# wo·w_in formed once on the chip; u and v taken from the 256 gated attention features; wo summed in the output's PSUM

## The chip, the cores and the metric

One core of one Trainium2 chip runs the whole kernel as one program. The metric is the device time of one execution in microseconds (us). TensorE (PE in the profile) multiplies, VectorE (DVE), ScalarE (ACT) and GpSimd (POOL) work element by element, and SyncE's queue (SP) issues nearly all DMAs. Each engine takes its instructions in the order in which they stand in its own queue; engines wait for one another by semaphores.

## The reference, cut to what matters

Eight batches of S = 576 tokens; D = 512 model features, E = 4 experts (heads) of 64, so 256 gated features per token.

```python
x = rmsnorm(q @ (k.T @ v)) * g_norm                  # 8 heads of 64 -> x[b] is 576 x 512
# attention over 4 experts, causal, top-2 gates w:
#   y[b] = sum_e w_e * softmax(mask(x wq_e (x wk_e)^T / 8)) (x wv_e) @ wo[e]
x2 = concat_e(w_e * a_e @ (x wv_e)) @ wo             # (576 x 256) @ (256 x 512)
h = gelu_tanh(x2 @ w_in)                             # (576 x 512) @ (512 x 1024)
u, v = h[:, :512], h[:, 512:]
vn = layernorm(v) * g_ln
gated = u * (w_sg @ vn + b_sg)                       # w_sg mixes the 576 tokens
out = x2 + gated @ w_out                             # (576 x 512) @ (512 x 512)
```

w_in and w_out arrive as 64-bit floats and are taken apart on the chip.

## The kernel before, in words

**Split products.** Nearly every matrix product takes three matmuls with fp32r operands: an operand is split into a rounded part (hi: a copy on ScalarE) and the rest (lo: a subtraction on VectorE or GpSimd), and hi·hi, hi·lo and lo·hi are summed in PSUM. Below, "a product" of 128 x 128 weights is three matmuls. A half row is 288 tokens.

**Phase 1** (class Phase1) runs per batch: front (the k·v products and the norm's sums, `kvps`, `outps`, `statps`), norm (`nps`), v and gates (`vps`), q and k (`qkps`), then attn: per head e = 0..3 and query block i = 0..4 scores (`scps`, L433 and L434), masked row minimum on VectorE (L436), exp on ScalarE (L448), transposes (`tps`, L483), their split (L491 ScalarE, L493 VectorE), `av` (`avps`, L510), and after each second head the gating of `gav` and its split into `gvh` (L530) and `gvl` (L531). `wo_out` (L534) multiplies these 256 gated features by wo (L543 to L545; 48 matmuls a batch), copies PSUM to `x2ev` on ScalarE (L546) and writes x2 to DRAM (`x2d`). The tag x2ev has two buffers and is shared by `x2ev` and by the `avt` of `av`.

**Order.** Each part is a generator with a time window in units of one batch's attention, relative to its batch (OPT["w"]: attn 0 to 1, wo 1.102 to 1.366, that is, during the next batch's first heads). `merge` calls the generators by these times, and a scheduler then sets each engine's order from this text order and its own estimate of times. The generator conv takes w_in, w_sg and w_out apart in pieces of 128 x 256 and stores hi and lo in DRAM over about six batches. Batch 7's attention is accompanied by `first` of Phase2.

**Phase 2** (class Phase2) takes the batches in pairs. `load_x` reads x2 back (`xraw`) and splits it (L739 ScalarE, L740 GpSimd). `upart` makes u over 512 features (L791 to L793; 96 matmuls a batch with 288 columns), `vpart` makes v in nine blocks of 128 tokens for a pair (L841 to L843; 108 matmuls a pair with 512 columns), each followed by gelu, batch statistics and `vnorm`. `spart` mixes tokens (L867 to L871; 112 a batch), multiplies by u and splits the result into `gh` and `gl`. `opart` multiplies by w_out (L899 to L901; 96 a batch), adds x2 read back once more (`xres`, L902) and writes the output. The weights of this phase lie where phase 1 keeps its attention tiles, so `Phase2.weights` can load them only when these are free.

Of the kernel before, what the change touches and what calls it, by code (L numbers as in the profile page):

```python
# [16 lines left out]
try:  # L17
# [17 lines left out]
P = 128  # L35
# [8 lines left out]
OPT = dict(ob=1, sx=0, pinq=0, dv=0, pin=1, cvb=2, xb=1, ldb=2, hp={}, n1=0, n2=0, f1=0, pa=4, sA=(), dg=0, cost=(1.01, 0.88, 1.22, 1.47, 1.28), avi=1, prb=4, ahb=2, alb=2, qkb=2, ahead=3, w={'attn': (0.0, 1.0), 'wo': (1.102, 1.366), 'qk1': (-0.013, 0.222), 'qk0': (-0.54, -0.204), 'v': (-0.683, -0.28), 'front': (-1.386, -0.923), 'norm': (-0.832, -0.787), 'conv': (0.032, 6.648), 'wts': (-1.938, -1.178), 'u': (0.319, 1.263), 'front_0': (-1.763, -1.646), 'v_0': (-1.478, -1.291), 'qk0_0': (-1.025, -0.914), 'qk1_0': (-0.003, 0.152), 'norm_0': (-1.6, -1.5)})  # L44
# [9 lines left out]
    "wo": [("attn", 0)],  # L54
# [12 lines left out]
class Phase1:  # L67
# [6 lines left out]
    def __init__(self, tc, late, early, ins, wts, x2d, nb):  # L74
        self.tc, self.nc, self.nb, self.x2d, self.wts = tc, tc.nc, nb, x2d, wts
        (self.qT, self.kvp, self.gn, self.wqkvg, self.wo, self.sel, self.bsel, self.mask, self.ident) = ins
# [58 lines left out]
    def consts(self):  # L135
# [24 lines left out]
        self.wohi = self.ac.tile([P, 2, D], F32R, name="wohi")  # L160
        self.wolo = self.ac.tile([P, 2, D], F32R, name="wolo")
# [3 lines left out]
    def weights(self):  # L165
        nc = self.nc
        for st, (n0, n1) in zip(self.stg, ((512, 772), (0, 256), (256, 512))):
            for c in range(NC):
                self.split(st[:, c, :], self.whi[:, c, n0:n1], self.wlo[:, c, n0:n1], -0.125 if n0 == 0 else None)
                yield 1.0  # L170
        nc.sync.dma_start(self.mask_sb, self.mask)
        nc.sync.dma_start(self.id_sb, self.ident)
        st = self.staging(2 * D).rearrange("p (r n) -> p r n", r=2)
        nc.sync.dma_start(st, self.wo.rearrange("(r p) n -> p r n", p=P))
        for r in range(2):
            self.split(st[:, r, :], self.wohi[:, r, :], self.wolo[:, r, :])
            yield 2.0
# [317 lines left out]
    def av(self, st, e):  # L495
# [7 lines left out]
        t = self.at.tile([P, S], F32, name="avt", tag="x2ev", bufs=2)  # L503
# [15 lines left out]
        if e % 2:  # L519
# [12 lines left out]
            st["gv"].append((hi, lo))  # L532

    def wo_out(self, b, st, c):  # L534
        nc = self.nc
        ev = self.at.tile([P, S], F32, name="x2ev", tag="x2ev", bufs=2)
        for h in range(2):
            r = slice(HF * h, HF * (h + 1))
            ps = self.bank("wops", True)[:, 0:HF]
            for k in range(2):  # L540
                hi, lo = st["gv"][k]
                wh, wl = self.wohi[:, k, c * P : (c + 1) * P], self.wolo[:, k, c * P : (c + 1) * P]
                nc.tensor.matmul(ps, wh, hi[:, r], start=(k == 0), stop=False)  # L543
                nc.tensor.matmul(ps, wh, lo[:, r], start=False, stop=False)
                nc.tensor.matmul(ps, wl, hi[:, r], start=False, stop=(k == 1))  # L545
            nc.scalar.copy(ev[:, r], ps)  # L546
        nc.sync.dma_start(self.x2d[b][c], ev)

    def attn(self, b, st):
        st["prob"], st["aT"], st["gv"], st["den"], st["R"] = {}, {}, [], [], []  # L550
# [3 lines left out]
        for n in range(len(steps) + ahead):  # L554
# [4 lines left out]
            if n >= ahead:  # L559
# [4 lines left out]
                if i == OPT["avi"] and e > 0:  # L564
                    with self.hp("a"):
                        self.av(st, e - 1)
                    yield 1.0
        self.av(st, E - 1)
        yield 1.0

    def wo_all(self, b, st):
        for c in range(NC):
            self.wo_out(b, st, c)
            yield 1.5
# [14 lines left out]
    def convert(self, w, src, hi_d, lo_d, rows, n):  # L589
        nc = self.nc  # L590
        new = lambda nm, dt, tag=None: self.cv.tile([P, 256], dt, name=nm, tag=tag or nm)[:, :n]
        if src.dtype == I64:
            x = new("cv_x", F32)
            xv = x[:rows]
            low, high = w[:rows, :, 0], w[:rows, :, 1]
            t = x.bitcast(U32)
            h, f = new("cv_h", U32), new("cv_f", F32)
            self.pin(nc.scalar.activation(f, low, AF.Copy, scale=2.0**-52))
            self.pin(
                nc.vector.tensor_scalar(t, high, 3, 0x3FFFFFF8, op0=OP.logical_shift_left, op1=OP.bitwise_and)  # L600
            )
            yield
            nc.vector.scalar_tensor_tensor(h, high, 0xC0000000, t, op0=OP.bitwise_and, op1=OP.bitwise_or)
            yield
            nc.vector.tensor_scalar(t, high, 0x7FFFFFFF, None, op0=OP.bitwise_and)
            yield
            nc.vector.scalar_tensor_tensor(
                x, t, float(897 << 20), h.bitcast(F32), op0=OP.is_ge, op1=OP.mult
            )
            yield  # L610
            nc.vector.tensor_scalar(h, t, 0xFF800000, None, op0=OP.bitwise_and)
            yield
            nc.gpsimd.tensor_tensor(f, f, h.bitcast(F32), op=OP.mult)
            nc.gpsimd.tensor_tensor(x, x, f, op=OP.add)
            yield
        else:
            xv = w[:rows]
            yield
        hi, lo = new("cv_hi", F32R, "cv_h"), new("cv_lo", F32R, "cv_f")
        self.pin(nc.scalar.copy(hi[:rows], xv))  # L620
        self.pin(nc.gpsimd.tensor_tensor(lo[:rows], xv, hi[:rows].bitcast(F32), op=OP.subtract))
        nc.sync.dma_start(hi_d.bitcast(F32), hi[:rows].bitcast(F32))
        nc.sync.dma_start(lo_d.bitcast(F32), lo[:rows].bitcast(F32))
        yield

    def conversions(self):
        units = []
        for src, hi, lo in self.wts:
            r, n = src.shape
            w = 192 if n == S else 256  # L630
            for r0 in range(0, r, P):
                r1 = min(r, r0 + P)
                for n0 in range(0, n, w):
                    n1 = min(n, n0 + w)
                    units.append([t[r0:r1, n0:n1] for t in (src, hi, lo)] + [r1 - r0, n1 - n0])
# [15 lines left out]
    def streams(self):  # L651
# [19 lines left out]
        prep.append((*w["wts"], 16.0, self.weights()))  # L671
# [18 lines left out]
class Phase2:  # L690


    def __init__(self, tc, ctx, ins, wts, x2d, out, nb):
        self.tc, self.nc, self.nb, self.x2d, self.out = tc, tc.nc, nb, x2d, out
        (self.g_ln, self.b_sg), (self.wi, self.ws, self.wo) = ins, wts
        left = lambda name, bufs, **kw: ctx.enter_context(tc.tile_pool(name=name, bufs=bufs, side="left", **kw))
        self.cu = left("m_cu", 1)
        self.xp = left("m_x", 1)
        self.up = left("m_u", 2)
        self.tp = left("m_t", 2)  # L700
        self.ps1 = left("m_ps1", 8 - OPT["pa"], space=PSUM)
        self.wih, self.wil = [], []

    def late(self, ctx):
# [3 lines left out]
        self.vp = right("m_v", 1)  # L708
        self.rp = right("m_r", 2)
# [6 lines left out]
    def load_wi(self, f):  # L716
        for lst, nm in ((self.wih, "h"), (self.wil, "l")):
            lst.append(self.cu.tile([P, NC, D], F32R, name=f"wi{nm}{f}"))
        for c in range(NC):
            for t, src in zip((self.wih[f], self.wil[f]), self.wi):  # L720
                self.move(t[:, c, :], src[c * P : (c + 1) * P, D * f : D * (f + 1)])
            yield 0.75

    def load_x(self, b):

# [303 lines left out]
```

## Time and profile before

| what | value |
|---|---|
| time, median of 3 runs | 979.5 us (977.41 to 980.55) |
| the profiled execution, its own time | 983.26 us |
| its span, first to last instruction | 981.4 us |
| mean granted TensorE clock | 0.979 |
| TensorE matmul busy | 926.1 us, 94% |
| VectorE busy | 551.6 us, 56% |
| ScalarE busy | 524.5 us, 53% |
| GpSimd busy | 372.1 us, 38% |
| DMA, mean over the span | 127 GB/s |

Busy shares are means over the span; phase 1 ends at about 573 us with the last `gvh`, and the shares on the two sides of it differ. The granted clock is a share of full speed. Matmuls are pipelined: the duration of one row overlaps the next row, so the cost of one in a dense stretch is the distance between starts.

### The profile page before, as it was taken

The page shows a single profiled execution, that of the slowest core. Times are in us where ns is not written, and L with a number is a line of the kernel's source. Part 1 is how long each engine was busy: PE and PEld are TensorE (multiplying, and loading weights), DVE is VectorE, ACT ScalarE, POOL GpSimd, SP SyncE. Part 2 cuts the span into 40 slices and gives each one's busy share as a digit, 9 for nine tenths or more (in the row PEclk, how much of TensorE's full clock was granted, in tenths as well). Part 3 has the DMA queues.
Part 4 walks back from the last instruction along what each step waited for, and adds up shares of the span by engine and source line. Part 5 has one row for each costly group of instructions (what it writes and reads, how often), then busy time and mean ns, then how long its engine had stood idle before and what let it go on. Part 6 is the DMA issues. An engine that isn't in the chain of part 4 may idle for free.

```text
span 981.4 us, 18531 instructions
## 1 busy us (share of the span) xinstructions
PE 926.1 (94%) x6592; PEld 877.0 (89%) x6592; DVE 551.6 (56%) x1551; ACT 524.5 (53%) x1386; POOL 372.1 (38%) x390
## 2 busy tenths in 40 slices
PE   5687999999899999999999998999999999999998
PEld 4577988899798988999898987998999999999998
DVE  4565868868797667887975527335222541246022
ACT  5376777677787868778756737213331243115200
POOL 0043555535454545456423313622172125323111
PEclk9698999999999999999999999999999999999999
DMA  9274563673654756634468118512032302330022
GB/s 278 79 196 116 142 197 111 198 211 108 179 169 142 217 155 190 188 112 134 129 161 291 34 41 275 156 54 74 1 105 90 97 1 63 108 97 2 1 95 76
DMA packets 79758, 124.41 MB, mean 127 GB/s; under 512 B 11489, under 2 KB 38945, under 8 KB 79666
## 3 DMA queue, kind: packets, MB, share of 16 engines
q1 hardware_dynamic: 79426, 122.83, 42.5%
q8 instruction: 53, 0.87, 0.4%
q0 software_dynamic: 240, 0.39, 0.2%
q14 instruction: 39, 0.32, 0.1%
HBM read 67.05 MB, written 27.82 MB: 97 GB/s over the span
## 4 chain that ended last, share of the span: by engine, by line
PE 73%; DVE 9%; ACT 8%; DMA 5%; issue 3%; SPq 2%; POOL 0%; ACTq 0%; DVEq 0%
PE avps L510 4%; PE ps L867 4%; PE ps L791 3%; PE ps L793 3%; PE ps L901 3%; PE ps L869 3%; PE ps L900 3%; PE ps L899 3%; PE ps L792 3%; PE ps L868 3%; PE ps L841 3%; PE ps L842 3%; PE ps L843 3%; PE tps L483 3%; PE qkps L297 3%
## 5 line engine op out<-in xcount | busy, mean ns | idle before, releaser
L448 ACT ACTIVATE prob<-prob,small 128x128 f32<-128x128 f32 (+4 forms) x160 | 97.7, 612 | 30.6 <-DVE small L436 28.9
L879 DVE TENSOR_TENSOR g<-ps,u 128x288 f32<-128x288 f32 (+2 forms) x80 | 30.3, 395 | 136.9 <-PE ps L871 136.8
L436 DVE CUSTOM_DVE_ANT_0 prob<-scps,mask_sb 128x128 f32<-128x128 f32 (+4 forms) x160 | 75.2, 478 | 40.1 <-PE scps L434 38.1
L493 DVE TENSOR_TENSOR aTl<-tps,aTh 128x384 fp32r<-128x384 f32 (+1 forms) x192 | 78.2, 431 | 20.0 <-ACT aTh L491 19.6
L883 POOL TENSOR_TENSOR gl<-g,gh 128x576 fp32r<-128x576 f32 x32 | 45.8, 1432 | 109.1 <-ACT gh L882 109.0
L882 ACT CAST gh<-g 128x576 fp32r<-128x576 f32 x32 | 21.6, 674 | 110.1 <-DVE g L879 109.8
L483 PE MATMUL tps<-id_sb,prob 96*128 96x96 f32 (+2 forms) x480 | 73.0, 263 | 6.4 <-ACT x2ev L546 3.3
L297 PE MATMUL qkps<-xhi,whi 128*128 128x288 f32 x256 | 78.3, 306 | 0.6 <-DVE bdl L212 0.4
L867 PE MATMUL ps<-wsh,vnh 128*128 128x288 f32 x256 | 75.4, 297 | 3.0 <-ACT wsl L763 3.0
L298 PE MATMUL qkps<-xlo,whi 128*128 128x288 f32 x256 | 76.5, 299 | 0.0
L299 PE MATMUL qkps<-xhi,wlo 128*128 128x288 f32 x256 | 76.1, 297 | 0.0
L793 PE MATMUL ps<-xh,wil 128*128 128x288 f32 x256 | 75.5, 296 | 0.0
L869 PE MATMUL ps<-wsh,vnl 128*128 128x288 f32 x256 | 75.5, 295 | 0.0
L792 PE MATMUL ps<-xl,wih 128*128 128x288 f32 x256 | 75.4, 296 | 0.0
L868 PE MATMUL ps<-wsl,vnh 128*128 128x288 f32 x256 | 75.3, 294 | 0.0
L901 PE MATMUL ps<-gh,wo2l 128*128 128x288 f32 x256 | 75.3, 295 | 0.0
L791 PE MATMUL ps<-xh,wih 128*128 128x288 f32 x256 | 74.4, 296 | 0.9 <-ACT xh L739 0.9
L900 PE MATMUL ps<-gl,wo2h 128*128 128x288 f32 x256 | 75.1, 294 | 0.0
L491 ACT CAST aTh<-tps 128x384 fp32r<-128x384 f32 (+1 forms) x192 | 68.9, 389 | 11.5 <-PE tps L483 10.6
L899 PE MATMUL ps<-gh,wo2h 128*128 128x288 f32 x256 | 73.7, 294 | 0.0
L433 PE MATMUL scps<-kh,qs 128*128 128x128 f32 (+2 forms) x192 | 64.8, 344 | 8.7 <-DMA kh<-hiT 4.0
L740 POOL TENSOR_TENSOR xl<-xraw,xh 128x576 fp32r<-128x576 f32 x32 | 46.6, 1461 | 63.6 <-ACT xh L739 59.3
(171 smaller groups left out, 3092.8 us busy)
## 6 DMA issues: line engine op xcount, KB each, us to landing
kv<-in_kvp SPq DMA_DIRECT2D x30, 384.0 KB, 4.1
kh<-hiT SPq DMA_DIRECT2D x64, 144.0 KB, 2.8
kl<-loT SPq DMA_DIRECT2D x64, 144.0 KB, 2.8
x2d<-x2ev SPq DMA_DIRECT2D x32, 288.0 KB, 2.8
xres<-x2d SPq DMA_DIRECT2D x32, 288.0 KB, 3.0
out<-oev SPq DMA_DIRECT2D x32, 288.0 KB, 2.2
q<-in_qT SPq DMA_DIRECT2D x30, 288.0 KB, 4.0
kv<-in_kvp SPq DMA_DIRECT2D x30, 192.0 KB, 4.3
```

The source lines that it names most:

```text
L297: nc.tensor.matmul(ps, whi, xhi, start=(c == 0), stop=False)
L448: nc.scalar.activation(sc[:m, 0:w], sc[:m, 0:w], AF.Exp, bias=mn, scale=-1.0, accum_out=den)
L483: nc.tensor.transpose(ps[:kr, m * j : m * j + m], pr[:m, _first(j) : _first(j) + kr], self.id_sb[:m, :m])
L791: nc.tensor.matmul(ps, wh, xh[:, c, :], start=(c == 0), stop=False)
L792: nc.tensor.matmul(ps, wh, xl[:, c, :], start=False, stop=False)
L793: nc.tensor.matmul(ps, wl, xh[:, c, :], start=False, stop=(c == NC - 1))
L867: nc.tensor.matmul(ps, vnh[:, j, fs], self.wsh[:, j, r], start=(j == 0), stop=False)
L868: nc.tensor.matmul(ps, vnh[:, j, fs], self.wsl[:, j, r], start=False, stop=False)
L869: nc.tensor.matmul(ps, vnl[:, j, fs], self.wsh[:, j, r], start=False, stop=False)
L899: nc.tensor.matmul(ps, wh, gh, start=(f == 0), stop=False)
L900: nc.tensor.matmul(ps, wh, gl, start=False, stop=False)
L901: nc.tensor.matmul(ps, wl, gh, start=False, stop=(f == NC - 1))
```

## The change

- `wo_out`, `wo_all`, their window and `x2d` go. `av` now writes `gvh` and `gvl` to DRAM (`gvd`), four transfers a batch, and `avt` has its own tag with two buffers.
- `conv` takes w_in apart as before, but keeps four fp32 pieces (`cv_x4`), multiplies them by the transposed wo (`wot`) in full fp32 (`wxps`, 32 matmuls with 256 columns in all), and stores hi and lo of the 256 x 1024 product. wo itself is split by the same generator (four pieces more).
- Phase 2 loads `gvh` and `gvl` as `xh` and `xl`, with no split. u and v now contract over 256 features: 48 matmuls a batch and 54 a pair. `opart` sums wo's six product terms and w_out's twelve in one PSUM bank (144 matmuls a batch) and copies it out; nothing is added or read back.
- `first` now makes the nine v blocks of batches 0 and 1 unprocessed (`raw`), then u of batch 0. After phase 1 come `vnorm` of these blocks and u of batch 1. `rest` then interleaves `spart` of b, `opart` of b - 1, v of the next pair and u of b + 1 step by step; vn has three buffers.
- The window of u is 0.25 to 1.0 (before 0.319 to 1.263), that of wts ends earlier.

The diff, cut to its core (conv's bit handling, loads and `vnorm` read as before):

```diff
-            st["gv"].append((hi, lo))
-    def wo_out(self, b, st, c):
...
-                nc.tensor.matmul(ps, wh, hi[:, r], start=(k == 0), stop=False)
-                nc.tensor.matmul(ps, wh, lo[:, r], start=False, stop=False)
-                nc.tensor.matmul(ps, wl, hi[:, r], start=False, stop=(k == 1))
-            nc.scalar.copy(ev[:, r], ps)
-        nc.sync.dma_start(self.x2d[b][c], ev)
+            for t, dst in zip((hi, lo), self.gvd[b]):
+                nc.sync.dma_start(dst[e // 2].bitcast(F32), t.bitcast(F32))
...
+            yield from self.whole(w, self.x4[:, c, :], rows)
+            if c < NC - 1:
+                return
+            for r in range(2):
+                rs = slice(r * P, (r + 1) * P)
+                ps = self.bank("wxps")[:, 0:256]
+                for j in range(NC):
+                    nc.tensor.matmul(ps, self.wot[:, j, rs], self.x4[:, j, :], start=(j == 0), stop=(j == NC - 1))
+                self.parts(ps, hi_d[rs, n0 : n0 + 256], lo_d[rs, n0 : n0 + 256], P, 256, psum=True)
...
+            for k in range(2):
+                wh, wl = self.wih[0][:, k, cols], self.wil[0][:, k, cols]
+                nc.tensor.matmul(ps, wh, xh[:, k, r], start=(k == 0), stop=False)
+                nc.tensor.matmul(ps, wh, xl[:, k, r], start=False, stop=False)
+                nc.tensor.matmul(ps, wl, xh[:, k, r], start=False, stop=(k == 1))
...
+            terms = [(self.woh[:, k, cs], self.wol[:, k, cs], xh[:, k, r], xl[:, k, r]) for k in range(2)]
+            terms += [
+                (self.wo2h[:, f, cs], self.wo2l[:, f, cs], gh[:, r], gl[:, r]) for f, (gh, gl) in enumerate(self.g[b])
+            ]
+            for n, (wh, wl, gh, gl) in enumerate(terms):
+                nc.tensor.matmul(ps, wh, gh, start=(n == 0), stop=False)
+                nc.tensor.matmul(ps, wl, gh, start=False, stop=False)
+                nc.tensor.matmul(ps, wh, gl, start=False, stop=(n == len(terms) - 1))
+            (nc.scalar.copy if h else nc.vector.tensor_copy)(ev[:, r], ps)
...
+        for k in range(9):
+            ps = self.vmat(0, k)
+            (nc.vector.tensor_copy if k % 2 else nc.scalar.copy)(self.raw[:, k, :], ps)
...
+        for k in range(9):
+            self.vnorm(0, k, self.raw[:, k, :])
+            if k in (1, 3, 5, 7):
+                f = k // 2
+                self.upart(1, f)
```

The scheduler's order moves with it. TensorE, batch 7's second head, before: its scores and transposes (`scps`, `tps`) have `wops` of batch 6 and the first u matmuls (`ps`) between them.

```order
L434 MATMUL scps<-kl_7714,qs_7519 128x128
L544 MATMUL wops<-gvl,wohi 128x288
L545 MATMUL wops<-gvh,wolo 128x288
L544 MATMUL wops<-gvl,wohi 128x288
L545 MATMUL wops<-gvh,wolo 128x288
L483 MATMUL tps<-id_sb,prob 128x128 x3
L543 MATMUL wops<-gvh,wohi 128x288
```

TensorE, the same head after the change:

```order
L428 MATMUL scps<-kl_7312,qs_7114 128x128
L477 MATMUL tps<-id_sb,prob 128x128 x3
L427 MATMUL scps<-kh_7311,qs_7114 128x256
L428 MATMUL scps<-kl_7312,qs_7114 128x256
L477 MATMUL tps<-id_sb,prob 128x96 x4
L427 MATMUL scps<-kh_7311,qs_7114 128x384
L428 MATMUL scps<-kl_7312,qs_7114 128x384
```

Nothing stands between the steps now, from the last q and k matmul in head 0 to the end of head 2; there the first v block (`ps` from `xh` and `wih`) begins.

TensorE after the change, where phase 1 has ended: the last v block that is made ahead (for batch 2) and the start of `spart` of batch 0, which reads the newly loaded `wsh` and `wsl` and the normed `vn`.

```order
L812 MATMUL ps_8634<-wil_7683,xh 128x512
L813 MATMUL ps_8634<-wih_7680,xl 128x512
L867 MATMUL ps_8425<-wsh,vn 128x288
L867 MATMUL ps_8441<-wsh,vn 128x288
L867 MATMUL ps_8488<-wsh,vn 128x288
L867 MATMUL ps_8504<-wsh,vn 128x288
L868 MATMUL ps_8425<-wsl,vn 128x288
```

Between the last matmul of the attention and these rows stand 24 u matmuls of batch 1 and 24 v matmuls of batch 2; before the change all 108 v matmuls of the first pair lie around this place.

TensorE after the change, one of the eight places of the new product in phase 1 (`wxps`, two groups of four matmuls for each 256 columns):

```order
L520 MATMUL rps<-id_sb,R 128x128
L610 MATMUL wxps<-cv_x_849,wot 128x256 x4
L520 MATMUL rps<-id_sb,R 128x96 x2
L427 MATMUL scps<-kh_1439,qs_1194 128x128
```

Its operand `cv_x` is the fourfold piece `cv_x4`; ahead of it and behind it stand the attention's own transposes and scores.

## Rows read from the trace of the kernel before

**Rows 1.** The page: busy us of each engine, share, instructions.
```profile
PE 926.1 (94%) x6592; PEld 877.0 (89%) x6592; DVE 551.6 (56%) x1551; ACT 524.5 (53%) x1386; POOL 372.1 (38%) x390
```
**Rows 2.** Stretches: length, then busy (count) of PE, PEld, DVE, ACT, POOL; clock, DMA.
```profile
0.00:120.00 120.00, 92.66 (x607) 83.25 (x608) 70.47 (x218) 70.49 (x197) 33.87 (x44) 0.90 0.57 161
120.00:520.00 400.00, 380.12 (x2882) 359.64 (x2881) 311.42 (x966) 299.90 (x884) 197.52 (x206) 0.98 0.58 164
520.00:600.00 80.00, 75.62 (x505) 70.31 (x504) 35.69 (x95) 49.69 (x122) 20.53 (x22) 0.98 0.42 139
600.00:960.00 360.00, 360.00 (x2473) 346.41 (x2472) 129.28 (x261) 103.09 (x183) 117.04 (x118) 1.00 0.24 74
```
**Rows 3.** TensorE in order of time, dense stretches: start, duration, what.
```profile
583.83 0.29 PE L543 MATMUL wops<-gvh,wohi 128*128 128x288 f32 x1
...
584.23 0.30 PE L543 MATMUL wops<-gvh,wohi 128*128 128x288 f32 x1
...
590.91 0.39 PE L841 MATMUL ps<-wih,xh 128*128 128x512 f32 x1
...
592.27 0.39 PE L841 MATMUL ps<-wih,xh 128*128 128x512 f32 x1
```
**Rows 4.** TensorE in order of time: fp32 products, transposes, and what follows each.
```profile
300.38 1.28 PE L206 MATMUL kvps<-kv 128*128 128x128 f32 x10
301.42 0.38 PE L297 MATMUL qkps<-xhi,whi 128*128 128x288 f32 x1
...
319.86 1.28 PE L483 MATMUL tps<-id_sb,prob 128*128 128x128 f32 x12
320.92 0.48 PE L247 MATMUL statps<-sqh,sel_sb 128*16 128x288 f32 x2
```
**Rows 5.** Who waited for whom: us, times, longest; then one such wait in time.
```profile
ACT x2ev L546 <- DMA x2d<-x2ev: 9.8, 6, 2.8
...
349.80 0.70 ACT L546 COPY x2ev<-wops 128x288 f32<-128x288 f32 x2 [2.79 <-DMA x2d<-x2ev]
...
350.25 0.44 PE L483 MATMUL tps<-id_sb,prob 128*128 128x128 f32 x2 [1.56 <-ACT x2ev L546]
```
**Rows 6.** Two stretches around that wait, columns as in rows 2.
```profile
345.00:350.00 5.00, 3.57 (x25) 3.10 (x24) 4.37 (x14) 2.21 (x6) 2.85 (x2) 1.00 0.93 245
350.00:355.00 5.00, 4.75 (x25) 4.65 (x26) 1.80 (x4) 3.15 (x8) 3.85 (x4) 0.66 0.26 99
```
**Rows 7.** ScalarE: the last gvh of batches 0 and 6.
```profile
132.88 0.66 ACT L530 CAST gvh<-gav 128x576 fp32r<-128x576 f32 x1
...
516.96 0.66 ACT L530 CAST gvh<-gav 128x576 fp32r<-128x576 f32 x1
```
**Rows 8.** Groups by line: busy, mean ns of one, idle before, releasers.
```profile
L448 ACT ACTIVATE prob<-prob,small 128x128 f32<-128x128 f32 (+4 forms) x160 | 97.7, 612 | 30.6 <-DVE small L436 28.9 <-DVE gden L364 0.7
L493 DVE TENSOR_TENSOR aTl<-tps,aTh 128x384 fp32r<-128x384 f32 (+1 forms) x192 | 78.2, 431 | 20.0 <-ACT aTh L491 19.6
L436 DVE CUSTOM_DVE_ANT_0 prob<-scps,mask_sb 128x128 f32<-128x128 f32 (+4 forms) x160 | 75.2, 478 | 40.1 <-PE scps L434 38.1 <-ACT prob L448 1.0
L491 ACT CAST aTh<-tps 128x384 fp32r<-128x384 f32 (+1 forms) x192 | 68.9, 389 | 11.5 <-PE tps L483 10.6
L448 ACT ACTIVATION_READ_ACCUMULATOR prob<-prob,small 128x1 f32 (+1 forms) x160 | 31.3, 196 | 0.0
L546 ACT COPY x2ev<-wops 128x288 f32<-128x288 f32 x64 | 23.7, 398 | 21.7 <-DMA x2d<-x2ev 9.8 <-PE wops L545 7.7 <-PE nps L282 2.5
```
**Rows 9.** The start of phase 2's weights and of spart, in order of time.
```profile
587.26 0.33 SPq L752 DMA_DIRECT2D glb<-in_g_ln  x1
...
596.80 1.30 PE L867 MATMUL ps<-wsh,vnh 128*128 128x288 f32 x4 [3.01 <-ACT wsl L763]
...
601.55 0.29 PE L868 MATMUL ps<-wsl,vnh 128*128 128x288 f32 x1
```

More of the change, by code (lines that the diff above doesn't have):

```diff
@@ L627, in conversions @@
         units = []
[L628 removed]
+        src, hi, lo = self.wts[0]
+        for n0 in range(0, 2 * D, 256):
+            for c in range(NC):
+                units.append([src[c * P : (c + 1) * P, n0 : n0 + 256], hi, lo, P, 256, (c, n0)])
+        for src, hi, lo in self.wts[1:]:
             r, n = src.shape
@@ new lines, in vmat @@
+    def vmat(self, p, k):
+        nc = self.nc
+        if k == 4:
+            (xh, xl), r = self.ends[p], slice(0, P)
+        else:
+            (xh, xl), j = self.x[2 * p + (k > 4)], k - 5 * (k > 4)
+            r = slice(j * P, (j + 1) * P)
+        ps = self.bank(self.ps1, "ps1")
+        for c in range(2):
+            wh, wl = self.wih[1][:, c, :], self.wil[1][:, c, :]
+            nc.tensor.matmul(ps, xh[:, c, r], wh, start=(c == 0), stop=False)
+            nc.tensor.matmul(ps, xh[:, c, r], wl, start=False, stop=False)
+            nc.tensor.matmul(ps, xl[:, c, r], wh, start=False, stop=(c == 1))
+        return ps
@@ new lines, in rest @@
+    def rest(self):
+        nb = self.nb
+        self.load_x(2)
+        self.load_x(3)
+        for k in range(9):
[3 more added lines that the diff above has]
+                self.upart(1, f)
+                ins = self.nc.scalar.activation(self.u[0][:, f, :], self.u[0][:, f, :], AF.Gelu_apprx_tanh)
+                self.tc.keep_in_program_order(ins)
+        for b in range(nb):
+            units = [(self.spart, b, 0)]
+            if b:
+                units += [(self.opart, b - 1, c) for c in range(NC)]
+            units += [(self.spart, b, f) for f in range(1, NC)]
+            p = b // 2 + 1
+            steps = []
+            if 2 * p < nb:
+                steps += [(n, self.vstep, p, k) for n, k in enumerate(range(4) if b % 2 == 0 else range(4, 9))]
+            if 0 < b < nb - 1:
+                steps += [(n + 0.5, self.upart, b + 1, f) for n, f in enumerate(range(NC))]
+            steps.sort(key=lambda t: t[0])
+            done = 0
+            for n, (fn, *args) in enumerate(units):
+                fn(*args)
+                if fn == self.opart and args[1] == NC - 1:
+                    self.load_x(b + 3)
+                while done < len(steps) * (n + 1) / len(units):
+                    _, step, *rest = steps[done]
+                    step(*rest)
+                    done += 1
+        for c in range(NC):
+            self.opart(nb - 1, c)
@@ L948, in fused_kernel, with vstep @@
+    def vstep(self, p, k):
+        if k == 0:
+            self.load_ends(p)
+        self.vnorm(p, k, self.vmat(p, k))
 @with_exitstack
-def fused_kernel(ctx, tc, qT, kvp, gn, wqkvg, wo, w_in, g_ln, w_sg, b_sg, w_out, sel, bsel, mask, ident, out):
+def fused_kernel(ctx, tc, qT, kvp, gn, wqkvg, woT, wo, w_in, g_ln, w_sg, b_sg, w_out, sel, bsel, mask, ident, out):
     nb = qT.shape[0]
     dp = ctx.enter_context(tc.tile_pool(name="x2dram", bufs=1, space=DRAM))
-    x2d = [dp.tile([NC, P, S], F32, name=f"x2d{b}") for b in range(nb)]
+    gvd = [[dp.tile([2, P, S], F32R, name=f"gv{x}{b}") for x in "hl"] for b in range(nb)]
@@ L960, in fused_kernel @@
     early.close()
-    ph2 = Phase2(tc, mlp, (g_ln, b_sg), [w[1:] for w in wts], x2d, out, nb)
+    ph2 = Phase2(tc, mlp, (g_ln, b_sg), [w[1:] for w in wts], gvd, out, nb)
     lo, hi = (nb - 1 + t for t in OPT["w"]["u"])
-    live = [[lo, step, gen] for lo, step, gen in left] + [[lo, (hi - lo) / 27.0, ph2.first()]]
+    live = [[lo, step, gen] for lo, step, gen in left] + [[lo, (hi - lo) / 19.2, ph2.first()]]
     merge([(lo, lo + step, 1.0, gen) for lo, step, gen in live])
```

431 lines of the change are left out of this document (179 added, 252 removed).

## The prediction

> **What bounds the kernel now.** First the page: TensorE's matmuls are busy for 94% of the span, VectorE and ScalarE for 56% and 53% [rows 1]. A mean over two phases says little, so next the busy time by stretches [rows 2]. From 600 to 960 us TensorE has no idle time at all, and the other engines are busy for about a third: phase 2 is TensorE's work and nothing else. From 120 to 520 us, inside phase 1, TensorE is busy 380.1 of 400 us, but VectorE 311.4 and ScalarE 299.9: it leads, with VectorE at 78% not far behind, and its clock is 0.98 of full speed. So a matmul removed in phase 2 is worth its full cost; one removed in phase 1 is worth it only as far as the queues can close the gap. Third, TensorE in order of time for the real cost of a matmul: three with 288 columns start within 0.40 us, six with 512 columns within 1.36 us [rows 3], so 0.133 and 0.227 us each.
>
> **The change, part by part.** All sums are made against the profiled execution (983.3 us, 1.9 us more than its span). It lies 3.8 us above the median of the runs, which I take off at the end.
>
> *Matmuls.* The wo product of phase 1 goes: 8 x 48 = 384 at 0.133, -51.2 us. u halves from 96 to 48 a batch: 384, -51.2. v halves from 108 to 54 a pair: 216 at 0.227, -49.0. The output product grows from 96 to 144 a batch: 384, +51.2. The new product is full fp32. The only fp32 products in the trace are `kvps`, where a matmul makes two rows: five matmuls of 128 columns take 1.04 us to the next start [rows 4], 1.63 ns a column. 32 x 256 = 8,192 columns make +13.3. Net: -86.9 us, of which -37.9 in phase 1 (wo and the new product) and -49.0 in phase 2.
>
> *Element work.* `x2ev` copies (64), the load splits (32 on ScalarE, 32 on GpSimd) and the residual's transfers go; 64 output copies replace the adds. In phase 2 this is hidden under TensorE, which has no idle time there [rows 2], so 0 both ways; uncovered, it would cost what the page's idle engines have to spare, and they have two thirds. In phase 1 ScalarE loses 23.7/8 = 3.0 us a batch [rows 8].
>
> *A stall that goes.* ScalarE waited 9.8 us in six pieces for `x2d` transfers to free `x2ev`; in the one shown, 2.79 us of it left TensorE idle for 1.56 us [rows 5] and the clock at 0.66 in the next 5 us [rows 6], about 1.6 us more. At that rate all six would be worth 11 us, at the least 0; I take -5. What is late next: `gvh` and `gvl` now wait for their own transfers, but each has two buffers and is made twice a batch, some 30 us apart, so nothing. SP's queue carries as many stores for them as for `x2d` (four a batch); for the weights it gets 16 stores fewer of the product than of w_in, and 4 loads and 8 stores more of wo: even, 0.
>
> *Phase 1 with less to fill it.* A batch takes (516.96 - 132.88)/6 = 64.0 us [rows 7]. TensorE is busy for 60.8 of it, and 60.8 - 6.4 + 1.9 (the new product, over seven batches) = 56.3 remains. If it is idle for 5% as now, a batch takes 59.3 us, with VectorE at 49.8 us (84%). The wo matmuls stood in the next batch's first heads as work that needs nothing from that attention, and the new product waits for a chain of ScalarE, VectorE and GpSimd; the scores behind it wait too. So I take 7% idle, 60.5 us: +1.2 x 7 = +8.5. Bounds: 0 (5% stays) and +33 (a batch stays at 64 us).
>
> *Batch 7's heads 0 to 2.* There the new order has no other work on TensorE. A head needs 3,712 score columns and 3,264 of `avps` at 0.133/288, 3.2 us, and 15 transposes at 1.06/12 [rows 4], 1.3: 4.5 us. ScalarE needs (97.7 + 31.3 + 68.9)/32 = 6.2 us a head, VectorE (75.2 + 78.2)/32 = 4.8, each before `av`'s evictions [rows 8]. 2.5 such heads leave TensorE idle for about 4 us more than before; with waits between the steps I take +5. Bounds: 0, and +16 if these 11 us of matmuls run at half clock besides.
>
> *The seam.* `spart` needs the newly loaded w_sg. Before, the first one began 9.5 us after the issue of `glb`, and the second operand was in use after 14.3 us; v matmuls covered all but 3.0 us of it [rows 9]. Now the cover behind the attention's last matmul is 24 x 0.133 + 24 x 0.227 = 8.6 us, and `glb` is issued about 2 us after that matmul, behind the last `gvh` and `gvl`: 16.3 - 8.6 is nearly 8 us idle, +5 against before. Bounds: +2 (GpSimd's part shorter, loads sooner) and +10 (with a lowered clock behind it). The extra changes of ScalarE's table in head 3 (gelu, exp, gelu) lie beside 18.6 us of v and u matmuls: 0, at the most +3.
>
> Sum: 983.3 - 86.9 - 5 + 8.5 + 5 + 5 = 909.9; less 3.8, **906 us**.
>
> [...]
>
> **The rivals.**
> *Full gain.* The scheduler fills what wo leaves, idle stays at 5%, the heads and the seam cost 2 us each: 983.3 - 86.9 - 5 + 4 - 3.8 = 892. For it: ScalarE gets lighter and the stall goes. Against it: the order shows the empty stretch of batch 7.
> *Phase 1 does not shrink.* VectorE's chain or the waiting product sets the pace, and a batch stays at 64 us: +33 instead of +8.5, 931 us. For it: in rows 6 VectorE is busy for 4.37 of 5 us while TensorE waits. Against it: over 400 us VectorE has 22% to spare [rows 2].
> [...]
> *It does not do what it says.* Excluded by the new order: 5,864 matmuls instead of 6,432, as counted above.
>
> **How the numbers follow.** The forecast (897 to 916) has 0.52; the full gain (below 897) 0.2; phase 1 that shrinks little or not (917 to 935) 0.24; slower 0.03; the remaining 0.01 lies between. No range can be told from no change within 0.3%, about 3 us; all cases but the last two are faster by far more, hence 0.96, 0.01, 0.03. The range 890 to 926 leaves out about 2 in 10, mostly above.
>
> **What would show it.** The part of phase 2 behind the seam should take about 33 us less: there 312 u matmuls and 186 v matmuls go (-41.5 and -42.2 us) and 384 of the output come (+51.2). If TensorE shows idle time there, the step "worth its full cost" is wrong. A batch between last `gvh` rows should be near 60 us; 64 means the third case, 58 the full gain. `wxps` rows should start 1.6 ns a column apart, with TensorE's idle time ahead of them under 1 us each. In heads 0 to 2 of batch 7 TensorE should be busy for about 60%, with the clock between 0.66 and 1. Between the last `gvh` and the first `spart` matmuls there should be about 8 us of idle time, released by w_sg's transfer or by `vn`. I would be wrong most of all if the granted clock of phase 1 falls below 0.95, or if VectorE has no idle time there.

## The result, and the profile after

The changed kernel takes 950.96 us (median of 4 runs, 946.42 to 954.41) beside 979.76 us (4 runs): a ratio of 0.9707, 95% interval 0.9657 to 0.9757. It is faster by 29 us; 74 were forecast, and the time lies above the range. All rows below are of its profiled run (946.42 us, span 944.6). The two profiled runs (983.26 and 946.42 us) lie 36.8 us apart, 8 more than the medians, so these rows show the change somewhat better than it is.

The page's line on the engines and its row of granted clocks in 40 equal slices of the span; the first answers to [rows 1]:
```profile
PE 863.8 (91%) x6056; PEld 808.5 (86%) x6056; DVE 540.9 (57%) x1513; ACT 500.8 (53%) x1321; POOL 317.0 (34%) x346
...
PEclk9699997988989999998999999799999999999999
```
Stretches, columns as in [rows 2]: inside phase 1, the seam, and phase 2 behind the last `gvh`.
```profile
120.00:520.00 400.00, 358.52 (x2547) 329.14 (x2546) 302.84 (x928) 274.86 (x801) 182.62 (x186) 0.94 0.53 150
...
580.00:592.80 12.80, 7.50 (x40) 6.20 (x38) 3.73 (x7) 7.46 (x15) 3.14 (x5) 1.00 0.68 213
...
580.10:944.60 364.50, 352.42 (x2513) 344.79 (x2511) 127.94 (x240) 111.61 (x209) 91.08 (x103) 0.99 0.18 60
```
ScalarE in order of time, the last `gvh` of batches 0, 6 and 7, as in [rows 7]:
```profile
128.73 0.68 ACT L524 CAST gvh<-gav 128x576 fp32r<-128x576 f32 x1
...
527.20 0.68 ACT L524 CAST gvh<-gav 128x576 fp32r<-128x576 f32 x1 [1.36 <-DVE gav L521]
...
580.12 0.67 ACT L524 CAST gvh<-gav 128x576 fp32r<-128x576 f32 x1
```
The last `gvh` cuts the result in two. Behind it the changed kernel needs 364.5 us; the kernel before needed 981.4 - 573.2 = 408.2. That is -43.7. Ahead of it the change gave nothing: 580.1 in place of 573.2 us, **+6.9**. In the profiles of all variants of the changed kernel below (every run but 4) the part behind the last `gvh` takes 364.1 to 366.7 us; so they differ ahead of it, and at the medians the +6.9 would be some +15 (an estimate: 43.7 less the 28.8 of the medians). A batch takes (527.20 - 128.73)/6 = 66.4 us, not the 60.5 forecast, and more than the 64.0 of [rows 7], although 48 matmuls a batch are gone.

From 120 to 520 us TensorE did 335 matmuls less than in [rows 2] and was busy for only 21.6 us less; its clock is 0.94 in place of 0.98: of 400 stretches of 1 us, 35 have a granted clock of 0.50, 350 one of 1.00 and 15 lie between (before 11, 381 and 8). Busy time times clock falls from 372.5 to 337 us, about 35. As an estimate from these rows, some 22 of them became waits, and the other 13 were eaten by the slower clock. What it waited for from 120 to 520 us (us, times, longest):
```profile
PE scps L427 <- DMA kh<-hiT: 9.9, 5, 3.0
PE scps L427 <- DVE small L430: 3.9, 5, 2.7
PE outps L227 <- DVE bdl L206: 3.2, 3, 1.3
PE qkps L291 <- ACT sq L229: 2.9, 3, 1.5
PE tps L477 <- DVE aTl L487: 2.7, 5, 1.5
```
No line of waits has more than a quarter of the 41.5 us: scores wait for `kh`, for VectorE's row minima, the front for VectorE and ScalarE. One such wait has the new product behind it. VectorE and TensorE in order of time:
```profile
198.48 1.26 DVE L574 SCALAR_TENSOR_TENSOR cv_h<-cv_w,cv_x 128x256 uint32<-128x256 uint32 x1 [2.25 <-DMA wd0h<-cv_hi]
199.66 0.41 DVE L430 CUSTOM_DVE_ANT_0 prob<-scps,mask_sb 128x256 f32<-128x256 f32 x1
...
200.01 1.16 DVE L576 TENSOR_SCALAR cv_x<-cv_w 128x256 uint32<-128x256 uint32 x1
...
200.14 0.73 PE L427 MATMUL scps<-kh,qs 128*96 128x512 f32 x1 [2.69 <-DVE small L430]
...
201.09 1.62 DVE L574 SCALAR_TENSOR_TENSOR cv_h<-cv_w,cv_x 128x256 uint32<-128x256 uint32 x1
...
203.38 0.45 PE L477 MATMUL tps<-id_sb,prob 128*128 128x128 f32 x1 [2.09 <-DVE gav L512]
```
And the stretch, columns as before, then all waits of VectorE for a store of the product (us, times, longest):
```profile
200.00:205.00 5.00, 2.74 (x8) 1.41 (x9) 4.91 (x10) 3.12 (x11) 2.43 (x2) 0.52 0.88 272
...
DVE cv_h L574 <- DMA wd0h<-cv_hi: 3.9, 3, 2.2
```
A finished group makes two high and two low parts in a row, in both buffers of `cv_h` and `cv_f`. The next piece's conversion needs those buffers, so VectorE stands for 2.25 us until a store has ended. The row minimum comes behind that wait and an operation of the conversion (1.26 us) in VectorE's queue, and TensorE waits 2.69 us for it. Two more operations of the conversion (1.16 and 1.62 us) stand ahead of the gating of `gav`, for which TensorE waits 2.09 us. The clock of that stretch is 0.52.

### The profile page after: what moved, and what is told of

Read it like the earlier page. It is cut to its first block, busy times and chain, and to the rows that moved or that the text cites. A ratio compares the mean times of both kernels' runs of the same rounds, so it can differ in the third digit from the quotient of the medians.

```text
span 944.6 us, 17150 instructions
## 1 busy us (share of the span) xinstructions
PE 863.8 (91%) x6056; PEld 808.5 (86%) x6056; DVE 540.9 (57%) x1513; ACT 500.8 (53%) x1321; POOL 317.0 (34%) x346
## 5 line engine op out<-in xcount | busy, mean ns | idle before, releaser
L427 PE MATMUL scps<-kh,qs 128*128 128x128 f32 (+2 forms) x192 | 71.8, 386 | 28.1 <-DMA kh<-hiT 14.0
L477 PE MATMUL tps<-id_sb,prob 96*128 96x96 f32 (+2 forms) x480 | 76.8, 273 | 7.5 <-DVE aTl L487 3.2
L867 PE MATMUL ps<-wsh,vn 128*128 128x288 f32 x256 | 76.3, 301 | 5.4 <-DMA wsh<-wd1h 5.4
L868 PE MATMUL ps<-wsl,vn 128*128 128x288 f32 x256 | 76.8, 300 | 2.8 <-DMA wsl<-wd1l 2.8
L869 PE MATMUL ps<-wsh,vn 128*128 128x288 f32 x256 | 76.4, 300 | 0.0
L427 PEld LDWEIGHTS scps<-kh,qs 128*128 128x128 f32 (+1 forms) x192 | 36.0, 192 | 39.7 <-DVE small L430 11.6
L477 PEld LDWEIGHTS tps<-id_sb,prob 96*128 96x128 f32 (+2 forms) x480 | 55.3, 147 | 17.0 <-issue 6.3
L872 DVE TENSOR_TENSOR g<-ps,u 128x288 f32<-128x288 f32 x64 | 28.8, 452 | 67.6 <-PE ps L871 67.6
L428 PE MATMUL scps<-kl,qs 128*128 128x128 f32 (+2 forms) x192 | 62.8, 344 | 1.8 <-DMA kl<-loT 1.6
L281 POOL TENSOR_TENSOR xlo<-o,xhi 128x576 fp32r<-128x576 f32 x28 | 39.9, 1436 | 71.4 <-ACT xhi L280 71.2
L504 PE MATMUL avps<-aTh,vst 128*128 128x320 f32 (+4 forms) x224 | 60.7, 291 | 1.5 <-DVE small L430 1.5
```

What stands on the lines that cost most here:

```text
L427: nc.tensor.matmul(ps, qs[:, q0 : q0 + m], kh[:, c0:c1], start=True, stop=False)
L477: nc.tensor.transpose(ps[:kr, m * j : m * j + m], pr[:m, _first(j) : _first(j) + kr], self.id_sb[:m, :m])
L867: nc.tensor.matmul(ps, vn[:, j, fs], self.wsh[:, j, r], start=(j == 0), stop=False)
L868: nc.tensor.matmul(ps, vn[:, j, fs], self.wsl[:, j, r], start=False, stop=False)
L869: nc.tensor.matmul(ps, vn[:, 5 + j, fs], self.wsh[:, j, r], start=False, stop=False)
```

## The experiments

Each run's time stands beside the kernel before on the same chip. The last three columns are from the trace of one profiled execution each, which lies up to 5 us from the median (run 5: 940.2 beside 935.0): the last `gvh`, the mean batch from batch 0's second `gvh` to batch 4's (the product's matmuls run until 318.6 us), and from there to batch 7's.

| kernel | us | ratio (95%) | last gvh | b 1-4 | b 5-7 |
|---|---|---|---|---|---|
| before | 979.8 | 1 | 573.2 | 65.4 | 59.6 |
| changed | 951.0 | 0.9707 (.9657-.9757) | 580.1 | 68.9 | 58.6 |
| 1 no product matmuls | 940.4 | 0.9603 (.9573-.9634) | 573.5 | 64.3 | 61.6 |
| 2 old conversion | 923.3 | 0.9428 (.9405-.9452) | 560.0 | 64.1 | 58.4 |
| 3 own buffers | 941.4 | 0.9614 (.9591-.9638) | 575.3 | 66.4 | 60.2 |
| 4 before, 1 of 6 wo | 974.4 | 0.9945 (.9920-.9970) | 567.8 | 65.3 | 58.6 |
| 5 less VectorE | 935.0 | 0.9563 (.9529-.9597) | 574.3 | 67.5 | 58.8 |
| 6 early q and k | 952.9 | 0.9738 (.9712-.9765) | 586.9 | 70.5 | 59.4 |
| 7 filler | 946.9 | 0.9682 (.9658-.9705) | 583.2 | 69.5 | 58.6 |
| 8 nudge | 946.2 | 0.9676 (.9660-.9692) | 576.7 | 70.2 | 56.0 |
| 9 = 1 and 3 | 945.5 | 0.9652 (.9633-.9672) | 578.3 | 66.1 | 60.4 |
| 10 = 3 and 7 | 943.4 | 0.9629 (.9599-.9658) | 576.9 | 68.4 | 58.2 |
| 11 = 3, early conversion | 935.8 | 0.9557 (.9530-.9583) | 568.3 | 64.8 | 57.9 |
| 12 = 3, banks 5 and 2 | 991.1 | 1.0116 (1.0087-1.0146) | 620.5 | 73.3 | 66.0 |
| 13 = 3, banks 3 and 4 | 966.4 | 0.9882 (.9828-.9936) | 597.9 | 67.2 | 62.3 |
| 14 = 3, product in attention's banks | 942.2 | 0.9641 (.9599-.9683) | 576.3 | 64.0 | 61.2 |
| 15 = 2 and 8 | 932.3 | 0.9532 (.9483-.9582) | 564.8 | 66.6 | 56.1 |
| 16 = 11 and 14 | 929.9 | 0.9512 (.9470-.9554) | 561.9 | 61.5 | 60.6 |
| 17 four banks for projections | 940.4 | 0.9594 (.9545-.9643) | 573.5 | 66.7 | 57.7 |
| 18 five banks for attention | 957.9 | 0.9780 (.9744-.9816) | 590.4 | 69.4 | 60.7 |

**1. The product without its matmuls.**
```diff
-                ps = self.bank("wxps")[:, 0:256]
-                for j in range(NC):
-                    nc.tensor.matmul(ps, self.wot[:, j, rs], self.x4[:, j, :], start=(j == 0), stop=(j == NC - 1))
+                ps = self.x4[:, r, :]
```


> The changed kernel without the 64 matmuls of the product: both parts of a finished group are taken from the converted pieces of w_in themselves, so the stores and every other instruction stay (the weights of u and v are then not the product). Cover theory (without the wo matmuls phase 1 is paced by transfers and VectorE, not by TensorE): the 15 us of these matmuls were no more than filler, and the time stays at 946 to 951 us. Conversion theory (the new product holds up batches 1 to 4), if its TensorE part is to blame: batches 1 to 4 fall from a mean of 68.9 us to some 64, and the time to about 931. If TensorE bounded phase 1, as the prediction had it: about 936, the 15 us of busy time.


It gave 10.6 us: between the theories, and nearest to the 936 us of the prediction's own.

**2. The old conversion.**
```diff
-            yield from self.whole(w, self.x4[:, c, :], rows)
...
+            x = self.cv.tile([P, 256], F32, name="cv_x", tag="cv_x")
+            yield from self.whole(w, x, rows)
+            rs = slice(c * P, (c + 1) * P)
+            self.parts(x, hi_d[rs, n0 : n0 + 256], lo_d[rs, n0 : n0 + 256], P, 256)
```


> The changed kernel with w_in converted as in the kernel before: each piece is split and stored by itself, GpSimd makes the low part, no piece is kept and nothing is multiplied (the weights of u and v are then two of the four row blocks of w_in, not the product). Conversion theory: batches 1 to 4 go back from a mean of 68.9 us to the 64.9 or less that they took before, and the time falls by 16 to 24 us to about 930. Cover theory: batches 1 to 4 stay within 2 us of what they are now and the time stays above 943. The prediction's own theory (TensorE is the bound): about 936.


27.7 us came back, more than any theory asked for.

**3. Own buffers for the product's stored parts.**
```diff
-        hi, lo = new("cv_hi", "cv_h"), new("cv_lo", "cv_f")
+        hi, lo = (new("cv_ph", "cv_x"), new("cv_pl", "cv_pl")) if psum else (new("cv_hi", "cv_h"), new("cv_lo", "cv_f"))
```


> The changed kernel with the stored parts of the product in buffers that the next piece's conversion does not need (high parts in the idle buffers of the later pieces, low parts in two new ones); it computes the same. Conversion theory, if the wait of VectorE for these stores is to blame: VectorE's waits for wd0h go, the stalls of scores behind them too, and the time falls by 6 to 15 us to 936 to 945. Cover theory: no change, 948 to 954.


9.5 us, inside the conversion theory's bounds. VectorE's waits for `wd0h` are gone from the trace; they were 3.9 us, so the rest is either what they held up or a new order of the queues (run 8).

**4. The kernel before with one wo matmul of six.**
```diff
-            for k in range(2):
...
+            hi, lo = st["gv"][h]
+            wh = self.wohi[:, h, c * P : (c + 1) * P]
+            nc.tensor.matmul(ps, wh, hi[:, r], start=True, stop=True)
```


> The kernel before with one matmul in place of six in each group of the output product in phase 1 (40 of 48 fewer a batch, 320 in all; the evictions, stores and loads stay, so x2 is not the full product). If TensorE bounds phase 1, as the prediction had it, 320 x 0.133 us = 42.6 us go, a batch falls from 64.0 to about 59 us, and the time to 937 to 945. Cover theory: the time that they took turns into waits of scores for kh and for VectorE; a batch stays at 62.5 us or more and the time at 968 or more.


320 matmuls less, 42.6 us by the row, brought 5.4 us. Its stretch:
```profile
120.00:520.00 400.00, 369.01 (x2620) 337.56 (x2620) 307.20 (x960) 299.27 (x884) 195.01 (x204) 0.94 0.59 163
```
Beside [rows 2], 262 matmuls are gone and only 11 us of busy time: one matmul counts as 141 ns of it in place of 132.

**5. VectorE relieved** of the operations at lines 574, 576 and 578.
```diff
-        nc.vector.scalar_tensor_tensor(h, high, 0xC0000000, t, op0=OP.bitwise_and, op1=OP.bitwise_or)
...
-        nc.vector.tensor_scalar(t, high, 0x7FFFFFFF, None, op0=OP.bitwise_and)
...
-        nc.vector.scalar_tensor_tensor(x, t, float(897 << 20), h.bitcast(F32), op0=OP.is_ge, op1=OP.mult)
```


> The changed kernel without three of the five VectorE operations on each of the 24 converted pieces (37.9 us of VectorE's time in phase 1; the converted weights are then other numbers). If VectorE sets the pace of phase 1 in place of TensorE: most of the 37.9 us come back and the time falls to 912 to 925 us. If the pace is set by chains of waits between the engines and by transfers for the scores, not by any engine's sum of work: 935 to 948. If TensorE bounded phase 1: no change, 948 to 954.


16 us of 37.9: VectorE's sum is at most a part of the pace.

**6. Earlier q and k.**
```diff
-'qk1': (-0.013, 0.222), 'qk0': (-0.54, -0.204)
+'qk1': (-0.113, 0.122), 'qk0': (-0.64, -0.304)
```


> The changed kernel with the windows of both halves of the q and k projections 0.1 of a batch earlier, nothing else. Third theory (what is left of phase 1 waits for kh because the projections stand right ahead of the scores that need them): TensorE's 14.0 us of waits for kh fall below 5 us and the time to 935 to 942. Conversion and cover theory: other waits take their place, 946 to 954.


From 80 to 520 us the waits for `kh` fell to 4.1 us, and waits for VectorE's `gav` (4.6) and `rr` (3.9) stand in their place. The third theory falls.

**7. The filler.**
```diff
+    def filler(self, b, st):
+        for c in range(NC):
+            for h in range(2):
...
+                    nc.tensor.matmul(ps, wh, hi[:, r], start=(k == 0), stop=False)
+                    nc.tensor.matmul(ps, wh, lo[:, r], start=False, stop=False)
+                    nc.tensor.matmul(ps, wl, hi[:, r], start=False, stop=(k == 1))
```


> The changed kernel with the 48 matmuls a batch of the old product put back in batches 0 to 6 at their old window, on the same tiles, their sums read by nobody (336 matmuls, 44.7 us at 0.133; no eviction, no store). Cover theory: they fill waits and keep the clock up, so the time stays within 6 us of 951. If TensorE bounds phase 1, as the prediction had it: all of it is added, 990 to 996. If half and half: about 973.


All 336 matmuls are back, and the kernel is not slower (946.9 beside 951.0). The clock is 0.97 from 120 to 520 us (0.94 in the changed kernel) and 1.00 from 320 us on (0.97 there):
```profile
120.00:520.00 400.00, 381.54 (x2875) 364.45 (x2874) 308.40 (x939) 278.29 (x808) 186.10 (x190) 0.97 0.54 155
...
320.00:520.00 200.00, 193.28 (x1513) 185.37 (x1512) 155.26 (x493) 148.79 (x439) 100.29 (x107) 1.00 0.58 167
```

**8. The nudge.**
```diff
-'v': (-0.683, -0.28)
+'v': (-0.673, -0.27)
```


> The changed kernel with one number of the plan nudged: the window of the v projection 0.01 of a batch later, some 0.6 us. No theory wants a change; whatever it shows (3 us or less expected, on either side of 951) is what a new order of the queues alone is worth, and the other runs are read against that, since each edit makes the scheduler order all queues anew.


Some 5 us, more than expected, for a new order of the queues alone; by itself this is not clear of the scatter, since the four runs of the changed kernel reach from 946.4 to 954.4. Run 15 beside run 2 shows 9 us for the same nudge, and there the runs lie clear of each other. So a difference of less than some 9 us between two kernels of this table tells nothing of a cause, and the 10 us of runs 1 and 3 are hardly more.

**9. Both cuts.** The edits of runs 1 and 3 together.

> Both earlier cuts of the product's cost together: own buffers for its stored parts, and its 64 matmuls left out (the weights of u and v are then not the product). If the two causes are separate, the gains of about 10 us each add: 929 to 933, and batches 1 to 4 take 62 to 64 us. If they are one cause seen twice, or half of each gain was a luckier order: 937 to 941.


They do not add: with both the kernel is 4 to 5 us slower than with either. Neither the matmuls nor the buffers can be called the cause by themselves.

**10. Own buffers and filler.**

> The changed kernel with own buffers for the product's stored parts and with the 336 filling matmuls put back. Cover theory: the filler is free here too, 937 to 943, as with own buffers alone. If there is less idle time to hide it in once the stores no longer hold VectorE: part of its 44.7 us shows, 950 or more.


Free again, beside run 3.

**11. The conversion started earlier**, on run 3.
```diff
-'conv': (0.032, 6.648)
+'conv': (-1.0, 6.648)
```


> Own buffers, and the conversion of the weights started a batch sooner, at -1.0 in place of 0.032 with the same end, so that two of the product's four groups fall into the first 120 us and VectorE's work for it is spread thinner. Conversion theory: batches 1 to 4 get shorter by some 2 us each and the time is 928 to 936, unless the startup gets longer by more than that. If it is the total of all work that counts: 939 to 944.


5.6 us against run 3, at the upper edge of the conversion theory's bounds: batches 1 to 4 get 1.6 us shorter each, batch 0 ends 6 us later. By run 8 a gain of this size shows no cause by itself.

**12. Five banks for the attention**, on run 3: `pa=5` in place of `pa=4`.

> Own buffers, and five PSUM banks for the attention in place of four, with two left for everything else in phase 1 (phase 2 gets five and three too). If the attention's batch of some 59 us behind the product is paced by banks that wait to be read, batches 5 to 7 fall to 56 us or less. If the projections' and the product's banks are what is short, phase 1 gets longer and the time is 950 or more. If neither: within 4 us of 941.


50 us slower than run 3; in the profiled runs all of it (45 us) lies ahead of the last `gvh`. TensorE's longest sums of waits, from 120 to 520 us:
```profile
PE scps L427 <- DMA kh<-hiT: 16.5, 5, 5.4
PE outps L225 <- DVE bdl L206: 8.2, 5, 2.5
```
The front's and the projections' work comes late, and the scores wait for `kh` from it.

**13. Three banks for the attention**, on run 3: `pa=3`.

> Own buffers, three PSUM banks for the attention and four for the projections, the front and the product (phase 2: three and five). If the banks of the projections pace phase 1: a batch gets shorter by 2 to 4 us and the time is 915 to 930. If the attention needs its four as much as the projections their three: 955 or more. If neither is short: within 4 us of 941.


25 us slower than run 3: the attention needs its four as well.

**14. The product in the attention's banks**, on run 3.
```diff
-                ps = self.bank("wxps")[:, 0:256]
+                ps = self.bank("wxps", True)[:, 0:256]
```


> Own buffers, and the product's sums in the attention's four banks in place of the projections' three. If the product's cost is that it takes one of three banks from the projections while ScalarE and VectorE come to empty it: batches 1 to 4 fall from 66 to about 64 us and the time to 925 to 934. If it is its place in the queues, whatever the bank: 938 to 946.


No gain by itself; what batches 1 to 4 gained was lost in batch 0 and in batches 5 to 7.

**15. The old conversion, nudged.**

> The conversion of w_in in its old form (no product, the weights of u and v other numbers) with the v projection's window 0.01 of a batch later, as in the nudged run before. If the 28 us of the old conversion are the product's cost: 920 to 928. If a good part of them was a luckier order of the queues: 932 to 940.


Against the changed kernel with the same nudge (946.2) the old conversion gives 13.8 us, against 27.7 without it. The product costs 14 to 28 us, and the order of the queues decides where in between.

**16. Runs 11 and 14 together.**

> Own buffers, the conversion started at -1.0, and the product's sums in the attention's banks; it computes the reference. If both help and add: 922 to 930. If the earlier start has already taken the product out of the crowded batches: 933 to 938, as with the earlier start alone.


It computes the same result and is faster than both kernels: 929.9 us, 21 less than the changed kernel and 49 less than the one before. Its stretch, to set beside that of the changed kernel above: 155 matmuls more in the same 400 us.
```profile
120.00:520.00 400.00, 373.82 (x2702) 342.80 (x2700) 304.28 (x975) 291.25 (x856) 185.51 (x188) 0.96 0.57 162
```
Whether the banks add to the earlier start is not settled: the intervals of runs 11 and 16 overlap, and their 6 us are no more than a new order may give.

**17. Four banks for the projections, none taken from the attention**: `sx=1` in the changed kernel.

> The changed kernel with the statistics' sums in short pieces in the projections' pool, which gets their bank: four banks for projections, front, product and statistics, the attention's four as they are (one ScalarE copy and three VectorE additions a batch more, some 1.6 us of work a batch). If the projections' banks pace phase 1: a batch gets 1 to 3 us shorter, the time 925 to 943. If three were enough for them: within 5 us of 949, the middle of the changed kernel and its nudge.


10.6 us against the changed kernel, 5.8 against its nudge: a fourth bank may help the projections' side, but that is not shown, since a new order may do nearly as much.

**18. That bank for the attention**: `sx=1`, `pa=5`.

> The same with that bank given to the attention: five there, three for projections, front, product and statistics. If the attention's banks pace phase 1: batches 5 to 7 fall below 57 us and the time to 925 to 943. If four were enough: 949 or, since the statistics now share the three, up to 965.


Slower by 7 us than the changed kernel: batches 5 to 7 did not fall below 57 us but rose. Nothing shows that the attention needs a fifth bank.

## Why the prediction was wrong

**The step that failed** is the one called phase 1 with less to fill it. It took the 64.0 us of a batch for TensorE's own (60.8 us busy and 5% idle) and so divided what busy time was left by 0.93. But TensorE's work did not set the batch. Runs 4 and 7 show it from both kernels: 320 wo matmuls taken from the kernel before are worth 5 us, and 336 put back into the changed one cost nothing. So of the -51.2 us for the wo product hardly anything came but the 6 us for batch 7, whose wo matmuls stand behind the last `gvh`, and the bound "a batch stays at 64.0 us" was the truth for that part. The clock can hide only a part of this: TensorE's busy time from 120 to 520 us at less than full clock is worth 358.5 x 0.06 = 21.5 us in the changed kernel and 381.5 x 0.03 = 11.4 in run 7, so of the filler's 44.7 us the higher clock may have given back some 10, and the other 35 went into waits (an estimate from these rows).

The reading error stands in [rows 2]. The stretch's 380.1 of 400 us is busy time of matmuls, and that did not shrink with the work: in run 4 nine per cent fewer matmuls are busy only three per cent less, at a lower clock (0.94) and with waits in between (a matmul that no other overlaps counts with all its 0.29 us, while in a dense stretch the next starts 0.133 us after it [rows 3]). The weight loads follow the missing work better: they were busy for 359.6 us (90%) in [rows 2] and for 337.6 (84%) in run 4. That too few PSUM banks are behind the waits is not shown: a bank taken from either side costs 50 and 25 us (runs 12 and 13), but one more gave no clear gain (17 and 18).

**The product** was the second part, a size: +13.3 us forecast, 14 to 28 measured (runs 2, 8 and 15). The matmuls' own price was right. All rows of `wxps` as a group, two for each of the 32 matmuls:
```profile
L610 PE MATMUL wxps<-cv_x,wot 128*128 128x256 f32 x64 | 15.1, 379 | 0.0
```
One of the eight groups of four, in order of time:
```profile
125.08 1.89 PE L610 MATMUL wxps<-cv_x,wot 128*128 128x256 f32 x8
126.81 0.33 PE L520 MATMUL rps<-id_sb,R 96*128 96x96 f32 x2
```
From the first start to the next row's it is 1.73 us for 1,024 columns, 1.69 ns a column for the 1.63 forecast (15.1 us is busy time, with each group's end), and TensorE is idle ahead of them for 0.0 us: my fear that it would stand there did not come true. One place where the product hurts is behind them, in VectorE's wait for the buffers shown above and in what that holds up; but these waits are 3.9 us in all. Of 20 us that phase 1 to the last `gvh` is longer than in run 2 (12 in the nudged pair), runs 1 and 3 got back 7 and 5, run 9 with both only 2; so the cost is shown, its division is not.

**Phase 2** was right, its sum in part by luck. I forecast -49.0 for its matmuls and +5 for the seam; the stretch behind the last `gvh` is 43.7 us shorter (TensorE's busy time -49.1, its idle time +5.4). By the rows of both traces 297 u, 250 v and 45 wo matmuls fewer lie in it and 384 of the output more, which at 0.133 and 0.227 us makes -51.2; the other 2 us I put down to the lower clock behind the seam (0.50, below). TensorE has no idle time from 600 to 940 us, and from `wsl`'s first use to the end it takes 944.6 - 597.0 = 347.6 us in place of 379.9, for the 33 us less that I named.

**The seam** was right in its idle time: 5.38 and 2.83 us, 8.2 for "about 8", released by w_sg's transfer, which is issued behind the last `gvh` and `gvl`, as [rows 9] let one expect. Two shifts nearly cancel in it: `glb` was issued some 6 us behind the attention's last matmul in place of 2, and the second operand was in use 12.5 us after that in place of 14.3.
```profile
584.47 0.33 SPq L753 DMA_DIRECT2D glb<-in_g_ln  x1
...
592.87 1.30 PE L867 MATMUL ps<-wsh,vn 128*128 128x288 f32 x4 [5.38 <-DMA wsh<-wd1h]
...
597.01 0.61 PE L868 MATMUL ps<-wsl,vn 128*128 128x288 f32 x1 [2.83 <-DMA wsl<-wd1l]
597.41 0.44 PE L869 MATMUL ps<-wsh,vn 128*128 128x288 f32 x1
597.65 0.44 PE L867 MATMUL ps<-wsh,vn 128*128 128x288 f32 x1
...
597.00:600.00 3.00, 2.99 (x12) 3.00 (x13) 2.97 (x6) 1.76 (x3) 2.41 (x4) 0.50 1.05 296
```
Behind these waits the granted clock is 0.50 until 602.9 us, and matmuls with 288 columns start 0.24 us apart in place of 0.133. By the distances of the starts that costs about 3.5 us, against 1.5 behind the shorter gap before the change; my +5 left it out, and only its upper bound had it.

**Batch 7** did not behave as I had it: not 60% busy in its first heads but 20.23 of 23 us from 527 us on, at a clock of 1.00 and not the half that my upper bound supposed (the trace before has 0.50 elsewhere, from 352 to 354 us), with 2.8 us idle (1.5 in the same stretch before), where I had added 5 for missing filler. It is 52.9 us long, 3.3 less than before. Its heads had wo matmuls of batch 6 between them before, so this fits run 7, but it is no test by itself.

**The stall of `x2ev`** went, as forecast; what it was worth can't be told apart from the rest of phase 1.

**The clock.** I wrote that I would be wrong most of all if phase 1 ran below 0.95; it runs at 0.94 from 120 to 520 us. The lower clock goes with the missing filler: run 7 brings it to 0.97, and to 1.00 from 320 us on, and the time stays. Whether the filler's own work used up the some 10 us that this can have given back (the estimate above), no run separates, so a part of that size by the clock is not excluded. The clock is low in the stall's stretch above (0.52), but the large loss is not by the clock: 44.7 us of matmuls put back cost no time. VectorE kept idle time (302.8 of 400 us busy).

**The rivals.** The case "phase 1 does not shrink" was the one that came, 931 us; the time is 20 us above it. Behind the last `gvh` the two agree, so these 20 lie ahead of it: batches 1 to 6 take 2.4 us longer each than the 64.0 of that case (14 us in the profiled runs). The product's cost beyond the forecast, 1 to 15 us, is part of it; the rest is not explained.

**What stays open** is which chain sets a batch in TensorE's place. It is not TensorE's sum of work (4, 7, 10), not the `kh` transfers alone (6), in part VectorE's work (5), and it needs three banks for the projections and four for the attention, with a fourth for the projections worth little (12, 13, 17, 18). No run took batches 5 to 7 below a mean of 56 us, and the order of the queues moves it by as much as most cuts.

## What to carry to other kernels

An engine that is 95% busy in a stretch need not bound it (here 380.1 of 400 us, and 320 matmuls less brought 5.4 us): put matmuls in that nobody reads, or take some out, and see whether the time moves, before pricing what a change removes there. Work that was taken from between two waits became a wait here, some 22 of 35 us by the estimate above. New work on the queue of an engine that others wait for can hold them up by the buffers that it shares, as VectorE's wait of 2.25 us for a store shows, with TensorE's of 2.69 us behind it, so look there and not only at the new work's own time. And in a kernel whose order a scheduler makes, nudge a number that no theory cares for first, to know what an order is worth.

## What the runs showed of the hardware

One VectorE operation of one shape took from 0.28 to 1.51 us. Line 580 of the changed kernel (ns, shortest, median, longest):
```profile
L580 DVE TENSOR_SCALAR cv_h<-cv_x x24: 275/293/1505, 63.5 to 514.1; 128x256 uint32<-128x256 uint32 x24
```
The long ones lie beside GpSimd's operations: 16 of these 24 overlap none and take 275 to 295 ns, the six that take over 0.5 us overlap one for 0.41 us or more, and the other two take 0.28 us although they overlap one too (by 0.27 us at 160.53). VectorE and GpSimd of the changed kernel in order of time:
```profile
60.20 1.42 POOL L232 TENSOR_TENSOR sql<-sq,sqh 128x576 fp32r<-128x576 f32 x1
...
62.50 0.29 DVE L576 TENSOR_SCALAR cv_x<-cv_w 128x256 uint32<-128x256 uint32 x1
...
63.92 0.73 POOL L582 TENSOR_TENSOR cv_f<-cv_f,cv_h 128x256 f32<-128x256 f32 x1 [2.30 <-DVE cv_h L580]
...
68.55 1.49 POOL L232 TENSOR_TENSOR sql<-sq,sqh 128x576 fp32r<-128x576 f32 x1 [1.08 <-ACT sqh L230]
...
68.86 1.34 DVE L576 TENSOR_SCALAR cv_x<-cv_w 128x256 uint32<-128x256 uint32 x1
```
Line 576 at 62.50 lies in a pause of GpSimd and takes 0.29 us; at 68.86 it starts within a GpSimd operation, takes 1.34 us and ends 0.16 us after it (68.55 + 1.49 = 70.04). The rows do not show why. If VectorE is held up by GpSimd in them, a part of its 302.8 busy us from 120 to 520 us is such waiting; that was not tried, nor what it costs the kernel.
